# Wider DMA transfers and one decay product in a delta-rule recurrence with two MoE stages behind it

## Chip, cores and metric

One core of a Trainium2 chip. The metric is the device time of one execution in microseconds (us). Before the change it is 1340.9 us, the median of 3 runs (1339.5 to 1342.97). Engines are named as the profile does: PE (matmul; PEld loads its weights), DVE (VectorE), ACT (ScalarE), POOL (GpSimd), SP (SyncE, which here only issues transfers).

## What is computed

The reference runs a recurrence over 768 time steps for 4 x 8 heads with a 40 x 40 state each, then a mixture of 8 experts with the top 2 of them, then a dense two-layer network:

```python
for t in range(S):                       # S = 768, D = 40
    y[:, :, t] = einsum('bhd,bhde->bhe', rt, state)
    Sa = einsum('bhde,bhe->bhd', state, at)
    state = state * wt[:, :, None, :] - einsum('bhd,bhe->bhde', Sa, bt)
    state = state + einsum('bhd,bhe->bhde', vt, kt)
x = y as (B * S, H * D) = (3072, 320)
x = moe(x)                               # softmax of the top 2 noisy logits, relu experts, d_ff 1024
out = (h * tanh(softplus(h))) @ w_out    # h = x @ w_in, d_ff 2048
```

## The kernel before

The recurrence is done in 24 chunks of C = 32 time steps. For each chunk `i`, `scale` (lines 217 to 243) forms on DVE the running products E of the decays w (a scan, line 224), their counterpart R (lines 227 and 228), then `abd`, the vectors a times E (line 235), and on POOL it multiplies k and b by R in place (`kb`, line 238). Two heads share the 128 partitions: one stands on rows 0 to 39, the other on rows 64 to 103 (`RW` = 104), the rows between hold zeros. `abd` holds each head in a plane of its own (index `ab`) with zeros in the rows of the other, so a product over all 104 rows gives one head's result. For chunks 0 to 3 (`nd` = 3) DVE makes abd, later POOL does, in two products of 40 x 512.

`prods` (lines 265 to 283) multiplies abd with k and b on PE: 8 head pairs times 4 products of 32 x 64, each over 104 rows, into four column strips of one PSUM bank. ACT copies the two halves out; one, `Ls`, is stored to DRAM as `lscr`. `turns` (289 to 313) transposes kb and the decays `Ec` on PE; ACT copies the first out as `kn`, which SP stores to DRAM as `knd` (line 303), and `load_kb` (469) later reads it back as the lower half of `KB`. `kn` has two buffers.

For each group of four chunks, `solve_group` (388 to 467) loads lscr as `Lu`, inverts 128 unit triangular 32 x 32 matrices at once, mostly on DVE (lines 414 to 429), and stores them as `tscr`, which `tbd` reads back in four transfers. `apply` (365) uses them for `Zt` (line 378). The chain (lines 586 to 620) then takes 48 steps (24 chunks times two of the four batches' pairs): `u_mm`, `s_mm`, `tr`, `rv_mm` and `y_mm`, each needing the state `ST` of the step before. `rv_mm` ends with DVE's `RR` (line 584), which `y_mm` reads (line 503).

The order on PE, ACT, DVE and POOL is the order in which the program emits it: `run` walks the chain and, between its parts, `pump` emits the next piece of preparing, solving and applying whose due time has come. Each engine works its list in order. SP's list is sorted by the scheduler; it issues nearly all transfers of this part, so a load that waits for its buffer holds up what is behind it. `pair` (line 199) splits the loads of wa (w and a) and kb: one transfer for chunks 0 to 3, later one for each head's 40 rows. Four buffers hold wa for chunks 0 to 3, two later; kb has three.

The experts and the dense network (from line 1100 on) begin as the chain ends; the change does not touch them.

Of the kernel before, what the change touches and what calls it, by code (L numbers as in the profile page):

```python
# [21 lines left out]
C = 32  # L22
# [7 lines left out]
NTB = 2  # L30
GJ = 4
RW = 64 + D


def layout_rec(inp):

    c = np.ascontiguousarray

    def heads_t(x):
        return x.reshape(NP, PR, 2, NC, C, D).transpose(3, 2, 5, 1, 0, 4)  # L40


    wa = np.zeros((NC, 2, 64, NW + 1 + 2 * PR * C), np.float32)
    w33 = np.ones((NC, 2, 64, PR, 2, C + 1), np.float32)
    w33[..., 0] = 0
    w33[:, :, :D, :, :, 1:] = heads_t(inp["w"])
    wa[..., :NW] = w33.reshape(NC, 2, 64, NW)
    wa[:, :, :D, NW + 1:] = heads_t(inp["a"]).reshape(NC, 2, D, -1)
    at = inp["a"].reshape(NP, PR, 2, NC, C, D).transpose(3, 0, 4, 2, 1, 5)
    kb = np.zeros((NC, 2, 64, PR, 2, 2, C), np.float32)  # L50
    for x, n in enumerate("kb"):
        kb[:, :, :D, :, :, x] = heads_t(inp[n])
    rt = inp["r"].reshape(NP, HH, NC, C, D).transpose(2, 4, 0, 1, 3)
    vn = np.zeros((NC, NP, C, HH, 64), np.float32)
    vn[..., :D] = inp["v"].reshape(NP, HH, NC, C, D).transpose(2, 0, 3, 1, 4)
    flat = lambda x: x.reshape(NC, 128, -1)
    rows = lambda x: c(flat(x)[:, :64 + D])
    return dict(wa=rows(wa), at=c(at).reshape(NC, 64, -1), kb=flat(kb), r=c(heads_t(inp["r"])).reshape(NC, 2, D, -1), rt=c(rt).reshape(NC, D, -1), vn=vn)


UR = (96, 32)
# [2 lines left out]
class Rec:  # L64
# [22 lines left out]
    def consts_a(self):  # L87
        nc, one = self.nc, self.one
        self.w33, self.wa, self.a, self.abd, self.kb = [], [], [], [], []

        self.kbs = [one.tile([128, 4 * HH * D], F32, name=f"KB{i}") for i in range(2)]
        n = NW + 1 + 2 * PR * C
        for i in range(4):
            t = one.tile([128, n], F32, name=f"wa{i}") if i < 2 else self.kbs[0][:, n * (i - 2):n * (i - 1)]
            self.wa.append(t)
            self.w33.append(t[0:RW, 0:NW + 1])
            self.a.append(t[:, NW + 1:].rearrange("p (a b c) -> p a b c", a=PR, b=2))
        for i in range(3):
            self.kb.append(one.tile([128, PR, 2, 2, C], F32, name=f"kb{i}"))
        self.kb3 = self.share[:, 6 * PR * 96:6 * PR * 96 + 4 * PR * C].rearrange("p (a b s c) -> p a b s c", a=PR, b=2, s=2)  # L100
        self.AT = one.tile([128, 2, PR, D], F32, name="AT")
        for i in range(GJ):
            self.load_w(i)
            self.load(i)
        self.zero = one.tile([128, 64], F32, name="zero")
        nc.gpsimd.memset(self.zero, 0.0)
        self.d1 = one.tile([128, 2 * PR, C + 1], F32, name="d1")
        nc.gpsimd.memset(self.d1, 0.0)
        nc.gpsimd.memset(self.d1[:, :, 0:1], -1.0)
        self.d1b = []  # L110
        for i in range(2):
            t = one.tile([128, 2 * PR * (C + 1) + 1], F32, name=f"d1b{i}")
            nc.vector.memset(t, 0.0)
            self.d1b.append(t)
            self.abd.append(one.tile([128, PR, 2, 2, C], F32, name=f"abd{i}"))
            nc.vector.memset(self.abd[i], 0.0)
        make_identity(nc, self.ident)

        self.mml = one.tile([128, C], F32, name="mml")
        nc.gpsimd.memset(self.mml, 0.0)  # L120
        for q in range(4):
            m = self.mml[32 * q:32 * q + 32]
            nc.gpsimd.affine_select(out=m, in_=m, pattern=[[1, C]], compare_op=ALU.is_ge,
                                    fill=1.0, base=0, channel_multiplier=-1)
        self.AM = [self.share[:, i * PR * 96:(i + 1) * PR * 96].rearrange("p (a x) -> p a x", x=96)
                   for i in range(2 * GJ)]
# [69 lines left out]
                nc.vector.memset(self.kbs[i][0:64], 0.0)  # L196


    def pair(self, out, x, i, rows=RW):

        for r in (slice(0, rows),) if i < GJ else (slice(0, D), slice(64, RW)):
            self.nc.sync.dma_start(out=out[r], in_=self.ins[x][i, r])

    def load_w(self, i):
# [7 lines left out]

    def load(self, i):

        self.pair(self.kbt(i).rearrange("p a b s c -> p (a b s c)"), "kb", i, rows=RW if i >= GJ else 128)

    def scale(self, i):

        nc = self.nc
        w, a, abd, kb = self.w33[self.wx(i)], self.a[self.wx(i)], self.abd[i % 2], self.kbt(i)[0:RW]  # L220
        E = self.p2.tile([128, PR, 2, C + 1], F32, name="E")
        R = self.p2.tile([128, NW + 2], F32, name="R")
        fl = E.rearrange("p a b c -> p (a b c)")
        nc.vector.tensor_tensor_scan(out=fl[0:RW], data0=w[:, 0:NW], data1=self.d1[0:RW].rearrange("p a b -> p (a b)"),
                                     initial=0.0, op0=ALU.mult, op1=ALU.add)
        d1b = self.d1b[i % 2]
        nc.vector.reciprocal(out=d1b[0:RW, C + 1::C + 1], in_=fl[0:RW, C::C + 1])
        nc.vector.tensor_tensor_scan(out=R[0:RW, NW::-1], data0=w[:, ::-1], data1=d1b[0:RW, ::-1],
                                     initial=0.0, op0=ALU.mult, op1=ALU.add)
        yield  # L230
        m = lambda t: t.rearrange("p a b s c -> p (a b) s c")
        Rv = R[0:RW, 2:NW + 2].rearrange("p (a c) -> p a c", c=C + 1)[:, :, None, 0:C]
        for ab in range(2):
            r = slice(64 * ab, 64 * ab + D)
            (nc.vector if i <= OPT['nd'] else nc.gpsimd).tensor_tensor(out=abd[r, :, :, ab], in0=a[r], in1=E[r, :, :, 0:C], op=ALU.mult)
        if GJ <= i + 2 < len(self.seq):
            self.load_w(i + 2)
        nc.gpsimd.tensor_tensor(out=m(kb), in0=m(kb), in1=Rv.to_broadcast([RW, 2 * PR, 2, C]), op=ALU.mult)
        we = self.pwe.tile([64, 2, PR, 2], F32, name="WE")
        nc.scalar.copy(out=we[0:D, :, :, 0].rearrange("p c a -> p a c"), in_=E[0:D, :, :, C])  # L240
        nc.scalar.copy(out=we[0:D, :, :, 1].rearrange("p c a -> p a c"), in_=E[64:64 + D, :, :, C])
        self.WE[i] = we
        self.scaled[i] = E
# [21 lines left out]
    def prods(self, i):  # L265
        self.made = i + 1

        nc = self.nc
        abd, kb, am = self.abd[i % 2][0:RW], self.kbt(i)[0:RW], self.AM[i % (2 * GJ)]
        fl = lambda t: t.rearrange("p s c -> p (s c)")  # L270
        if i % GJ == 0:
            self.lscr[i // GJ] = self.pd.tile([GJ * PR, 4, C, C], F32, name="lscr")
        pt = self.pp.tile([128, 512], F32, name="pp")
        for p in range(PR):
            for q in range(4):
                ab, c = divmod(q, 2)
                nc.tensor.matmul(pt[32 * q:32 * q + 32, p * 64:p * 64 + 64], lhsT=abd[:, p, c, ab], rhs=fl(kb[:, p, c]),
                                 start=True, stop=True, tile_position=(0, 32 * q))
        ls = self.p2.tile([128, PR, C], F32, name="Ls")

        for out, k in ((ls, 1), (am[:, :, 64:96], 0)):
            nc.scalar.mul(out=out, in_=pt.rearrange("p (q s x) -> p q s x", s=2, x=C)[:, :, k], mul=-1.0)
        (nc.scalar if i < OPT['dl'] else nc.sync).dma_start(out=self.lscr[i // GJ][i % GJ * PR:i % GJ * PR + PR].rearrange("u q t i -> (q t) u i"), in_=ls)
# [5 lines left out]
    def turns(self, i):  # L289
# [6 lines left out]
        for sg in range(2):  # L296
# [2 lines left out]
            for p in range(4):  # L299
                flip(pt[:, p * 128:p * 128 + RW], kb[0:RW, sg * 4 + p].rearrange("p b s c -> p (b s c)"))  # L300
            nc.scalar.copy(out=kn[:, sg * 8:sg * 8 + 8], in_=half(pt))
        self.KN[i] = self.pkn.tile([64, 2 * HH * D], F32, name="knd")
        (nc.scalar if i < OPT['dk'] else nc.sync).dma_start(out=self.KN[i].rearrange("r (c x) -> c r x", c=2), in_=kn.rearrange("p h d -> p (h d)"))
        if i % 2 == 0:
            self.EN[i // 2] = self.pen.tile([128, 2, PR, D], F32, name="EN")
        en, r0 = self.EN[i // 2], 64 * (i % 2)
# [162 lines left out]
    def load_kb(self, i):  # L469

        KB, kn = self.KB[i % 2], self.KN.pop(i)
        self.nc.sync.dma_start(out=KB[64:128, :, 0].rearrange("p c h d -> p c (h d)"), in_=kn.rearrange("p (c x) -> p c x", c=2))

    def copy_kb(self, g):
        t = self.KB[(g // NP) % 2][64:128, g % NP]
# [7 lines left out]

    def load_r(self, i):
        nc, ins = self.nc, self.ins
        nc.sync.dma_start(out=self.R2[i % 2][0:D].rearrange("p c h t -> p (c h t)"), in_=ins["rt"][i])

    def load_rbd(self, i):
        nc, ins = self.nc, self.ins
        if True:  # L490
            for ab in range(2):
                nc.sync.dma_start(out=self.rbd[i % 2][64 * ab:64 * ab + D, ab].rearrange("p a b c -> p (a b c)"), in_=ins["r"][i, ab])

    def y_mm(self, g, sg):
        nc = self.nc
# [1211 lines left out]
```

## Time and profile before

| | us |
|---|---|
| median of 3 runs | 1340.9 |
| profiled execution | 1343.39 |
| its span | 1341.6 |
| PE busy in the span | 1160.1 (86%) |
| DVE busy | 870.0 (65%) |
| ACT busy | 704.2 (52%) |
| POOL busy | 647.1 (48%) |

Three parts can be told apart: the start, until the first product of L378 at 111.16 us; the chain of 48 steps, until some 520 us; then the experts and the dense network, where PE is the bound. Shares of the whole span mix these three, so the stretches are read one by one. A granted clock of 1.00 is 2.4 GHz, 0.50 is 1.2 GHz. A DMA share of 1 means that all 16 DMA engines of the core are busy.

### The profile page before, as it was taken

Reading aid. Unit: us, or ns where it says so; the run is one execution under the profiler, and the core shown is the slowest. Engines: PE = TensorE matmul, PEld = TensorE weight load, DVE = VectorE, ACT = ScalarE, POOL = GpSimd, SP = SyncE. Lnnn points to the kernel's source line nnn. Section 1 sums busy time; section 2 is a strip of 40 time slices with the busy share of each in tenths; the row PEclk is TensorE's granted clock in tenths of the full one; section 3 lists DMA queues with packets and bytes.
Section 4 is the critical chain, followed back from the end, with each engine's and each line's share of the span. In section 5 each row is a group of like instructions: output and inputs, shape, how many; then the busy total and the mean of one; then the engine's idle time right before and its main releaser. Section 6 shows DMA issues by size and latency. Waiting matters only on the chain. (4 is left out here: it accounts for less than half of the span.)

```text
span 1341.6 us, 34128 instructions
## 1 busy us (share of the span) xinstructions
PE 1160.1 (86%) x13902; PEld 1111.0 (83%) x13902; DVE 870.0 (65%) x1579; ACT 704.2 (52%) x1477; POOL 647.1 (48%) x575
## 2 busy tenths in 40 slices
PE   3436787988688888899999999898889999999998
PEld 2335776877577877798999999898889999999998
DVE  8585939777594742755787786777356655666543
ACT  3423665756556555442443443443266676766664
POOL 4673855747473505542244443433256454554331
PEclk9657898989889988899999999999999999999999
DMA  5444465555525648463545645635281111110000
GB/s 147 144 122 124 131 173 148 148 159 151 143 81 128 112 98 123 127 177 120 153 122 159 188 143 170 216 104 180 72 216 31 31 41 40 30 31 16 16 11 21
DMA packets 140898, 152.48 MB, mean 114 GB/s; under 512 B 69646, under 2 KB 112654, under 8 KB 140718
## 3 DMA queue, kind: packets, MB, share of 16 engines
q1 hardware_dynamic: 123502, 116.17, 32.5%
q0 software_dynamic: 10752, 22.32, 6.1%
q10 hardware_dynamic: 6464, 11.54, 3.1%
q8 instruction: 120, 1.97, 0.7%
q14 instruction: 60, 0.49, 0.1%
HBM read 106.85 MB, written 43.12 MB: 112 GB/s over the span
## 5 line engine op out<-in xcount | busy, mean ns | idle before, releaser
L1579 POOL TENSOR_TENSOR gl<-fh,gh 128x1024 fp32r<-128x1024 f32 x46 | 131.0, 2876 | 105.2 <-ACT gh L1595 101.9
L1234 PE MATMUL ph<-xh,w1h 128*128 128x256 f32 (+1 forms) x576 | 160.9, 292 | 11.6 <-issue 10.5
L1234 PE MATMUL ph<-xl,w1h 128*128 128x256 f32 (+1 forms) x576 | 160.5, 291 | 0.0
L1547 PE MATMUL fps<-fxh,ih 128*128 128x256 f32 x576 | 156.3, 286 | 1.9 <-DVE fh L1549 1.9
L1547 PE MATMUL fps<-fxl,ih 128*128 128x256 f32 x576 | 153.7, 281 | 0.5 <-DVE fxl L1090 0.3
L1578 DVE TENSOR_TENSOR fh<-fh,fp 128x1024 f32<-128x1024 f32 x48 | 95.0, 2014 | 60.3 <-ACT fp L1577 60.3
L1253 PE MATMUL py<-w2h,hh 128*128 128x320 f32 x400 | 129.9, 325 | 2.7 <-ACT hh L1086 1.9
L1253 PE MATMUL py<-w2l,hh 128*128 128x320 f32 x400 | 125.7, 314 | 2.0 <-DVE w2l L1090 1.9
L1253 PE MATMUL py<-w2h,hl 128*128 128x320 f32 x400 | 125.9, 315 | 1.3 <-DVE hl L1088 1.3
L1088 DVE SCALAR_TENSOR_TENSOR hl<-ph,hh 128x512 fp32r<-128x512 f32 (+1 forms) x104 | 69.2, 665 | 87.5 <-ACT hh L1086 87.2
L1234 PEld LDWEIGHTS ph<-xh,w1h 128*128 128x128 f32 x576 | 112.4, 195 | 12.7 <-issue 12.6
L1549 DVE COPY fh<-fps 128x512 f32<-128x512 f32 x96 | 64.8, 689 | 79.4 <-ACT fp L1548 74.1
L1609 PE MATMUL fpy<-oh,gl 128*128 128x320 f32 x384 | 114.6, 310 | 0.0
L1609 PE MATMUL fpy<-oh,gh 128*128 128x320 f32 x384 | 114.3, 310 | 0.0
L1609 PE MATMUL fpy<-ol,gh 128*128 128x320 f32 x384 | 113.9, 308 | 0.0
L1234 PEld LDWEIGHTS ph<-xl,w1h 128*128 128x128 f32 x576 | 112.5, 195 | 0.4 <-DVE xl L1090 0.3
L1234 PE MATMUL ph<-xh,w1l 128*128 128x256 f32 (+1 forms) x384 | 111.7, 291 | 0.4 <-DVE w1l L1090 0.4
L1547 PEld LDWEIGHTS fps<-fxh,ih 128*128 128x128 f32 x576 | 109.0, 189 | 2.3 <-DVE fh L1549 2.2
L1547 PEld LDWEIGHTS fps<-fxl,ih 128*128 128x128 f32 x576 | 109.0, 189 | 1.1 <-DVE fxl L1090 1.1
L1547 PE MATMUL fps<-fxh,il 128*128 128x256 f32 x384 | 107.8, 281 | 0.0
L1086 ACT ACTIVATE hh<-ph 128x512 fp32r<-128x512 f32 (+1 forms) x104 | 60.0, 581 | 90.9 <-PE ph L1234 89.9
L1548 ACT ACTIVATE fp<-fps 128x512 f32<-128x512 f32 x96 | 56.1, 597 | 79.0 <-PE fps L1547 74.9
(273 smaller groups left out, 3342.1 us busy)
## 6 DMA issues: line engine op xcount, KB each, us to landing
share<-in_w_dram SPq DMA_DIRECT2D x9, 1280.0 KB
share<-in_w_dram SPq DMA_DIRECT2D x9, 1024.0 KB
knd<-kn SPq DMA_DIRECT2D x24, 320.0 KB
KB<-knd SPq DMA_DIRECT2D x24, 320.0 KB
yb<-y SPq DMA_DIRECT2D x22, 320.0 KB
wa<-in_wa_dram SPq DMA_DIRECT2D x40, 162.7 KB
kb<-in_kb_dram SPq DMA_DIRECT2D x40, 160.0 KB
ST<-in_vn_dram SPq DMA_DIRECT2D x48, 128.0 KB
```

Of the source, the lines that this page charges most:

```text
L1086: nc.scalar.activation(out=hi, in_=src, func=AF.Relu if relu else AF.Copy)
L1088: nc.vector.scalar_tensor_tensor(out=lo, in0=src, scalar=0.0, in1=hi.bitcast(F32), op0=ALU.max, op1=ALU.subtract)
L1234: nc.tensor.matmul(ph[:, m % c], lhsT=a, rhs=b, start=(q == 0), stop=(q == len(ops) - 1))
L1253: nc.tensor.matmul(py, lhsT=a[:, m, ts], rhs=b[:, m], start=(m == 0 and q == 0), stop=(m == FC - 1 and q == 2))
L1547: nc.tensor.matmul(ph[:, i], lhsT=a, rhs=b, start=(q == 0), stop=(q == len(ops) - 1))
L1548: nc.scalar.activation(out=p[:, 2 * m2:2 * m2 + 2], in_=ph, func=AF.Sigmoid, scale=-1.0)
L1549: nc.vector.tensor_copy(h[:, 2 * m2:2 * m2 + 2], ph)
L1578: mul = lambda s: nc.vector.tensor_tensor(out=h[:, s], in0=h[:, s], in1=p[:, s], op=ALU.mult)
L1579: low = lambda s: (nc.vector if last and s.start % 8 else nc.gpsimd).tensor_tensor(out=gl[:, s], in0=h[:, s], in1=gh[:, s].bitcast(F32), o ...
L1609: nc.tensor.matmul(py, lhsT=a[:, m, ts], rhs=w[:, m], start=(q == 0), stop=(q == len(ops) - 1))
```

## The change

The store of `knd` has 128 rows of 640 numbers on both sides; before, its outermost size was 2 (the two chunks halves `c`), with 64 rows below it. `load_kb` reads it with `c` taken from the rows. The loads of wa, kb, r and rt carry 48 rows for each head (`DL` = 48) in place of 40, the additional ones zeros, and the four loads of wa in the head 112 rows in place of 104. `abd` has no planes any more: one product over all 104 rows makes it, on DVE for every chunk. `prods` multiplies each head's own 40 rows, at row 0 or 64.

```diff
+DL = 48
-    rows = lambda x: c(flat(x)[:, :64 + D])
+    rows = lambda x: c(flat(x)[:, :64 + DL])
+    pad = lambda x: np.concatenate([c(x), np.zeros((*x.shape[:-4], DL - D, *x.shape[-3:]), np.float32)], -4)
...
-            self.abd.append(one.tile([128, PR, 2, 2, C], F32, name=f"abd{i}"))
-            nc.vector.memset(self.abd[i], 0.0)
+            self.abd.append(one.tile([128, PR, 2, C], F32, name=f"abd{i}"))
...
-    def pair(self, out, x, i, rows=RW):
-        for r in (slice(0, rows),) if i < GJ else (slice(0, D), slice(64, RW)):
+    def pair(self, out, x, i, rows=64 + DL):
+        for r in (slice(0, rows),) if i < GJ else (slice(0, DL), slice(64, 64 + DL)):
...
-        for ab in range(2):
-            r = slice(64 * ab, 64 * ab + D)
-            (nc.vector if i <= OPT['nd'] else nc.gpsimd).tensor_tensor(out=abd[r, :, :, ab], in0=a[r], in1=E[r, :, :, 0:C], op=ALU.mult)
+        nc.vector.tensor_tensor(out=abd[0:RW], in0=a[0:RW], in1=E[0:RW, :, :, 0:C], op=ALU.mult)
...
-        abd, kb, am = self.abd[i % 2][0:RW], self.kbt(i)[0:RW], self.AM[i % (2 * GJ)]
+        abd, kb, am = self.abd[i % 2], self.kbt(i), self.AM[i % (2 * GJ)]
...
-                nc.tensor.matmul(pt[32 * q:32 * q + 32, p * 64:p * 64 + 64], lhsT=abd[:, p, c, ab], rhs=fl(kb[:, p, c]),
-                                 start=True, stop=True, tile_position=(0, 32 * q))
+                r = slice(64 * ab, 64 * ab + D)
+                nc.tensor.matmul(pt[32 * q:32 * q + 32, p * 64:p * 64 + 64], lhsT=abd[r, p, c], rhs=fl(kb[r, p, c]),
+                                 start=True, stop=True, tile_position=(64 * ab, 32 * q))
...
-        self.KN[i] = self.pkn.tile([64, 2 * HH * D], F32, name="knd")
-        (nc.scalar if i < OPT['dk'] else nc.sync).dma_start(out=self.KN[i].rearrange("r (c x) -> c r x", c=2), in_=kn.rearrange("p h d -> p (h d)"))
+        self.KN[i] = self.pkn.tile([128, HH * D], F32, name="knd")
+        (nc.scalar if i < OPT['dk'] else nc.sync).dma_start(out=self.KN[i], in_=kn.rearrange("p h d -> p (h d)"))
...
-        self.nc.sync.dma_start(out=KB[64:128, :, 0].rearrange("p c h d -> p c (h d)"), in_=kn.rearrange("p (c x) -> p c x", c=2))
+        self.nc.sync.dma_start(out=KB[64:128, :, 0].rearrange("p c h d -> p c (h d)"), in_=kn.rearrange("(c p) x -> p c x", c=2))
```

`load_r` and `load_rbd` load `DL` rows in place of `D` in the same way.

How the lists move: on DVE a product for abd follows each R. The piece is DVE's list around the scans of chunks 4 and 5, in the start; `wa`, `d` and `d1b` are inputs of the scans, `P` and `tm` belong to the solving. Before:

```order
L224 SCALAR_TENSOR_TENSOR E<-wa_139,d_155 104x528
L227 RECIPROCAL d1b_158<-E 104x16
L228 SCALAR_TENSOR_TENSOR R<-wa_139,d1b_158 104x529
L429 TENSOR_REDUCE P<-tm 128x64
L224 SCALAR_TENSOR_TENSOR E<-wa_140,d_155 104x528
L227 RECIPROCAL d1b_162<-E 104x16
L228 SCALAR_TENSOR_TENSOR R<-wa_140,d1b_162 104x529
```

The same place with the change:

```order
L225 SCALAR_TENSOR_TENSOR E<-wa_139,d_155 104x528
L228 RECIPROCAL d1b_158<-E 104x16
L229 SCALAR_TENSOR_TENSOR R<-wa_139,d1b_158 104x529
L234 TENSOR_TENSOR abd_160<-wa_139,E 104x512
L429 TENSOR_REDUCE P<-tm 128x64
L225 SCALAR_TENSOR_TENSOR E<-wa_140,d_155 104x528
L228 RECIPROCAL d1b_161<-E 104x16
L229 SCALAR_TENSOR_TENSOR R<-wa_140,d1b_161 104x529
```

Only the row of L234 is new; the rest of DVE's list keeps its order.

On POOL both products of each chunk go. The piece is POOL's list from the end of the head to chunk 6; `share` is the tile that holds the decayed a of `scale_a` (L262) and the masked products (L287). Before:

```order
L287 TENSOR_TENSOR share<-share,mml 128x8x32 x4
L262 TENSOR_TENSOR share<-AT,EN 64x8x40 x6
L235 TENSOR_TENSOR abd_160<-wa_139,E 40x16x32 x2
L238 TENSOR_TENSOR kb_142<-kb_142,R 104x1024
L262 TENSOR_TENSOR share<-AT,EN 64x8x40 x2
L131 MEMSET share 128x16x24
L235 TENSOR_TENSOR abd_164<-wa_140,E 40x16x32 x2
L238 TENSOR_TENSOR kb_143<-kb_143,R 104x1024
```

The same place with the change:

```order
L287 TENSOR_TENSOR share<-share,mml 128x8x32 x4
L261 TENSOR_TENSOR share<-AT,EN 64x8x40 x6
L237 TENSOR_TENSOR kb_142<-kb_142,R 104x1024
L261 TENSOR_TENSOR share<-AT,EN 64x8x40 x2
L132 MEMSET share 128x16x24
L237 TENSOR_TENSOR kb_143<-kb_143,R 104x1024
```

The kb products (L238, now L237) stand directly behind `scale_a`. The lists of PE, ACT and SP keep their order.

## Rows read from the trace of the kernel before

**Rows 1.** The page, the span in 40 equal slices, PE and its clock
```profile
PE   3436787988688888899999999898889999999998
...
PEclk9657898989889988899999999999999999999999
```
**Rows 2.** Stretches (us): busy time of each engine, granted clock, DMA share, GB/s
```profile
core 0: us, PE busy (x) PEld busy (x) DVE busy (x) ACT busy (x) POOL busy (x), PEclk, DMA share, GB/s
...
111.00:530.00 419.00, 348.13 (x7488) 316.60 (x7488) 279.52 (x471) 252.68 (x700) 228.29 (x195) 0.90 0.56 134
530.00:1342.00 812.00, 772.84 (x5793) 763.17 (x5792) 511.02 (x1029) 414.48 (x693) 347.95 (x282) 0.98 0.35 100
```
**Rows 3.** Short stretches of the start, same columns
```profile
17.50:18.00 0.50, 0.37 (x12) 0.14 (x12) 0.47 (x2) 0.00 (x0) 0.00 (x0) 1.00 0.77 251
23.00:23.50 0.50, 0.09 (x2) 0.09 (x4) 0.50 (x1) 0.00 (x0) 0.36 (x1) 1.00 0.61 242
...
61.00:64.00 3.00, 1.62 (x8) 1.06 (x7) 0.00 (x0) 0.61 (x2) 2.54 (x3) 0.50 0.13 51
```
**Rows 4.** Timeline of SP's transfers in the start: issue, us, what
```profile
99.02 0.36 SPq L463 DMA_DIRECT2D tscr<-Tt  x1
99.47 0.57 SPq L303 DMA_DIRECT2D knd<-kn  x1
```
**Rows 5.** Waits of the start (total us, times, longest), and PE's first L378
```profile
DVE E L224 <- DMA wa<-in_wa_dram: 13.1, 1, 13.1
DVE E L224 <- ACT Ec L248: 3.2, 1, 3.2
ACT kn L301 <- DMA knd<-kn: 12.1, 5, 4.7
...
111.16 3.70 PE L378 MATMUL pp<-Tbd,share 128*96 128x128 f32 x16 [14.19 <-DMA kb<-in_kb_dram]
```
**Rows 6.** PE's waits from 111 to 530 us: total us, times, longest
```profile
PE pp L378 <- DMA Tbd<-tscr: 10.7, 4, 4.5
PE cs L528 <- issue: 8.3, 2, 4.7
PE cs L528 <- DMA ST<-in_vn_dram: 8.1, 3, 3.7
PE cs L528 <- DVE RR L584: 7.3, 5, 2.3
...
PE Y L503 <- DVE RR L584: 5.1, 3, 2.6
```
**Rows 7.** Timeline from 193 to 207 us, PE and DVE
```profile
193.93 1.31 PE L503 MATMUL Y<-KB,RR 128*32 128x40 f32 x32
...
202.86 0.17 DVE L414 TENSOR_TENSOR tm<-Tt,Lu 128x4 f32<-128x4 f32 x1 [10.94 <-DMA Lu<-lscr]
...
206.59 2.34 PE L503 MATMUL Y<-KB,RR 128*32 128x40 f32 x32 [2.61 <-DVE RR L584]
```
**Rows 8.** Groups by line and shape: busy us, mean ns | idle before
```profile
L235 POOL TENSOR_TENSOR abd<-wa,E 40x512 f32<-40x512 f32 x40 | 62.4, 1560 | 33.5 <-DMA ST<-in_vn_dram 16.1 <-PE cs L558 9.4 <-PE cs L541 2.1
...
L228 DVE TENSOR_TENSOR_SCAN R<-wa,d1b 104x529 f32<-104x529 f32 x22 | 40.5, 1841 | 1.5
...
L228 DVE TENSOR_TENSOR_SCAN R<-KB,d1b 104x529 f32<-104x529 f32 x2 | 2.5, 1259 | 0.2
```
**Rows 9.** Timeline of chunk 3: both abd, and POOL's kb
```profile
26.77 0.66 DVE L235 TENSOR_TENSOR abd<-KB,E 40x512 f32<-40x512 f32 x1
...
27.46 2.55 DVE L235 TENSOR_TENSOR abd<-KB,E 40x512 f32<-40x512 f32 x1
...
26.93 2.52 POOL L238 TENSOR_TENSOR share<-share,R 104x1024 f32<-104x1024 f32 x1 [3.57 <-DVE R L228]
```
**Rows 10.** L's products on PE: the group, and one block
```profile
L277 PE MATMUL pp<-kb,abd 104*32 104x64 f32 x1472 | 32.9, 250 | 35.1 <-POOL kb L238 34.8
...
190.54 1.10 PE L277 MATMUL pp<-kb,abd 104*32 104x64 f32 x64
```

More of the change, by code (lines that the diff above doesn't have):

```diff
@@ L56, in layout_rec @@
     flat = lambda x: x.reshape(NC, 128, -1)
-    rows = lambda x: c(flat(x)[:, :64 + D])
-    return dict(wa=rows(wa), at=c(at).reshape(NC, 64, -1), kb=flat(kb), r=c(heads_t(inp["r"])).reshape(NC, 2, D, -1), rt=c(rt).reshape(NC, D, -1), vn=vn)
+    rows = lambda x: c(flat(x)[:, :64 + DL])
+    pad = lambda x: np.concatenate([c(x), np.zeros((*x.shape[:-4], DL - D, *x.shape[-3:]), np.float32)], -4)
+    return dict(wa=rows(wa), at=c(at).reshape(NC, 64, -1), kb=flat(kb), r=pad(heads_t(inp["r"])).reshape(NC, 2, DL, -1), rt=pad(rt).reshape(NC, DL, -1), vn=vn)
 UR = (96, 32)
@@ L213, in load @@
     def load(self, i):
-        self.pair(self.kbt(i).rearrange("p a b s c -> p (a b s c)"), "kb", i, rows=RW if i >= GJ else 128)
+        self.pair(self.kbt(i).rearrange("p a b s c -> p (a b s c)"), "kb", i, rows=128)
     def scale(self, i):
@@ L485, in load_r @@
         nc, ins = self.nc, self.ins
-        nc.sync.dma_start(out=self.R2[i % 2][0:D].rearrange("p c h t -> p (c h t)"), in_=ins["rt"][i])
+        nc.sync.dma_start(out=self.R2[i % 2][0:DL].rearrange("p c h t -> p (c h t)"), in_=ins["rt"][i])
     def load_rbd(self, i):
@@ L491, in load_rbd @@
             for ab in range(2):
-                nc.sync.dma_start(out=self.rbd[i % 2][64 * ab:64 * ab + D, ab].rearrange("p a b c -> p (a b c)"), in_=ins["r"][i, ab])
+                nc.sync.dma_start(out=self.rbd[i % 2][64 * ab:64 * ab + DL, ab].rearrange("p a b c -> p (a b c)"), in_=ins["r"][i, ab])
     def y_mm(self, g, sg):
```

## The prediction

> **What bounds the kernel now.** I read the 40 slices of 33.5 us first [rows 1]: from the 18th on PE is mostly busy at 0.9 and more; in the first four it is at 0.3 to 0.6, and its clock falls to 0.5; between them it is at 0.6 to 0.9. The stretches say the same in microseconds [rows 2]: from 530 us to the end PE works 772.84 of 812 us, and none of that work is touched. From 111 to 530 us (the 48 steps of the chain) it works 348.13 of 419 us at a mean clock of 0.90, so some 71 us are idle. So what the change is worth is decided before 530 us, and what is won there moves the rest forward as a whole.
>
> What the early part waits for stands in the DMA share. From 61 to 64 us, as in other stretches behind the stores of **knd**, the share is 0.13 at 51 GB/s [rows 3]: 0.13 of 16 engines is two engines, at some 25 GB/s each. A store of 320 KB at 51 GB/s takes 327,680 B / 51 GB/s = **6.4 us**, there are 24 of them, 154 us in all, and every later transfer that also needs those two engines stands behind. The loads of 40 rows show the same thing milder: while only they run, share 0.61 and 242 GB/s [rows 3], that is ten engines. The waits name who pays [rows 5]: in the start VectorE waits 13.1 us for a load of `wa`, and 3.2 us for ScalarE's copy `Ec`, which itself sits behind `kn` copies that wait 12.1 us for knd stores. PE's first product of the chain waits 14.2 us, up to 111.16 us [rows 5], though its source `tscr` was stored at 99.02; directly behind that store SP issued a knd store [rows 4].
>
> **The change, part by part. knd over all engines.** Both sides of the store are now 128 rows of 2,560 B. The nearest row for a wide transfer is that of the head [rows 3]: 251 GB/s at a share of 0.77. At that rate a store takes 1.3 us in place of 6.4. The bounds: 51 GB/s (nothing changes) and 16 x 25 = 400 GB/s (0.8 us). I take 1.3, since the other transfers share the engines. The 40-row loads become 48-row loads: a fifth more bytes, but three rows on each of 16 engines in place of four on each of ten, if 48 spreads over 16, which no row shows. The Trainium skill, "DMA: Bandwidth & Descriptors", section "Why a DMA increments its semaphore by 16 and not by 1", says that the engine count is the largest up to 16 that divides the outermost sizes; by it 48 and 128 go over 16, and two engines for knd and ten for 40 rows agree with the shares above.
>
> *The start.* VectorE's waits of 13.1 and 3.2 us are 16.3 [rows 5]. The wa load will be issued at about the same place in SP's list, whose order does not change, and land behind one knd store: 1.3 us, and 1.6 for its own 400 KB at 251 GB/s, so I keep 3 us of wait: **-13**. From tscr's store to PE's start it took 111.16 - 99.02 = 12.1 us, with one knd store among the transfers between; it gives back at most 6.4 - 1.3 = 5.1, and I take **-3.5**. Bounds for both: 0, if POOL or ScalarE is as late, and -16.3 - 5.1.
>
> *The chain.* From 111 to 530 us PE's waits with a transfer at the end are 10.7 us for Tbd and 8.1 for ST [rows 6]; the 8.3 of "issue" may be transfers too, for nothing that the profile shows was missing. One more is a DMA in disguise: at 202.86 us VectorE gets Lu after 10.94 us and begins the L414 ladder; the RR product that PE wants stands behind it, PE is idle 2.61 us up to 206.59, and then the 32 products L503 take 2.34 us where they took 1.31 at 193.93 [rows 7]: after the hole PE runs at its lower clock. RR is 7.3 + 5.1 us of PE's waits [rows 6]. So 10.7 + 8.1 = 19 us are sure to belong to DMA, 8 more are likely and 12 possible: 39; and the lower clock behind a hole costs about 1 us for each block like that of L503, perhaps 18 us over six large holes with three such blocks each (an estimate). Bounds 0 and 39 + 18; I take **-26**, the 19 sure ones and 7 of the rest, since the next thing (POOL's kb, ScalarE's copies) will be late at some of these places.
>
> **abd in one product, on VectorE.** Per stage, two POOL products of 1.56 us go (62.4 us in all [rows 8]) and VectorE gets one of 104x512. On VectorE two of 40x512 stand in each of the first four stages; the first takes 0.66 us, the second 2.55 [rows 9]: the second begins beside POOL's kb product (26.93, 2.52 us) and ends when that has ended. The new one is like the first, for it stands directly behind R, and kb waits for R too: 20 x 0.66 = 13 us added. Against it stands R: 1.26 us in the head, where POOL makes no abd, and a mean of 1.84 over the 22 others [rows 8]; without abd on POOL it falls by 0.58 x 20 = 11.6. Sum on VectorE **0**; bounds +51 (20 abd behind a kb, 2.55 each) and -12. That POOL's 62 us go is worth nothing by itself, since POOL works 228.29 of 419 us in the chain [rows 2] and is waited for seldom; but kb comes two abd, some 3 us, earlier in each stage. If kb takes its turn first, the next late thing is RR, and PE waits for it.
>
> *The head.* VectorE is busy throughout a stage of the head, with E, R and two abd. One abd goes, but E of the next stage now meets kb as the second abd did, so only the first one's 0.66 us is sure; bounds 0.66 and 2.55 [rows 9] a stage, for three stages. I take the lower: **-2**. The two memsets of abd stood while wa was awaited: nothing.
>
> **L's products on 40 rows.** 32 products a stage stay 32, each on 40 rows at row 0 or 64 in place of 104. A block of 64 instructions takes 1.10 us, though an instruction takes 250 ns in the mean [rows 10]: they overlap over four column strips. No row shows a product that starts at row 64. Fewer rows do not shorten a product whose columns are the same: **0**. The Trainium skill says against it ("TensorEngine Tiling (Array Packing)", section "Restrictions and Gotchas") that different row tiles cannot access the same PSUM bank at the same time; here both halves write one bank. By rows 10 the sum stays; by that rule it is the slow rival below.
>
> **Sum.** -13 - 3.5 - 26 + 0 - 2 + 0 = **-44.5**. The profiled execution took 1343.39 us (span 1341.6 and 1.8 around it), 2.5 above the median of 1340.9; 1343.4 - 44.5 = 1299. Against the median it would be 1296. I say **1298**.
>
> **The rivals.**
> - *Only the start gains* (0.17). The chain's order is fixed, and each hole closed by a faster store may open again for ScalarE, VectorE or POOL; for it: PE's 12.4 us of waits for RR [rows 6] and VectorE at 279.52 of 419 us [rows 2]. Then -18.5: 1325.
> - *All holes close and the clock with them* (0.15). For it: the clock of 0.90 in the chain against 0.98 later [rows 2]. Start -21, chain -39, clock -18, head -2: 1343 - 80 = 1263, say 1270 with something left.
> - *Slower: the halves take turns in PSUM* (0.08). Place: the 16 stages whose products lie in the chain. Each block changes its row half 16 times; if each change waits for an instruction to end (250 ns [rows 10]), a block costs 16 x 0.25 = 4.0 us more, 64 us in the chain, where PE is the bound, with the other 8 blocks hidden in the start. 1299 + 64 = 1363. It decides from 44.5 / 16 = 2.8 us a block. Against it: the halves use different columns and partitions.
> - *The stores do not spread* (0.04). Both sides must have 128 rows outermost as issued; if not, 1341: only the head gains 2 us.
>
> **How the numbers follow.** The forecast has 0.56, with a range of its own of 1283 to 1314; with all holes closed 0.15, only the start 0.17, slower 0.08, no spread 0.04. The range that leaves out no more than 2 in 10 takes in 'only the start' and most of 'all holes': **1268 to 1328**. A measurement of this kernel tells about 0.3%, 4 us, from no change. Faster 0.88, same 0.04, slower 0.08.
>
> **What would show it.** Right: no stretch at share 0.13 and 51 GB/s in the first 500 us; VectorE's wait for wa under 4 us; the first product of L378 near 92 us in place of 111; ScalarE's wait for knd gone; R near 1.26 us and abd on VectorE near 0.66; the block of L's products still 1.1 us at full clock; the gap between the first L378 and the end smaller by some 26 us. Wrong: a block over 2.8 us; abd over 2 us with PE's waits for RR above 12 us; new waits on PE for kb or `share` that take the place of those for Tbd and ST.

## The result, and the profile after

The changed kernel takes **1309.64 us** (median of 4 runs, 1307.29 to 1311.88), the kernel before beside it 1341.93: a ratio of **0.9755** [0.9722, 0.9789]. The direction and the range of the prediction hold; 1298 was 12 us too low. The profiled execution took 1308.13 us (span 1306.3) in place of 1343.39: 35.3 us less, where the sum said 44.5.

The page of the changed kernel, the 40 slices (now of 32.7 us), PE and its clock:

```profile
PE   3538888889789787998999999899989999999998
PEclk9559989999889799999999999889999999999999
```

Its stretches (columns as in [rows 2]). The third stands near the end of the chain and is needed further down:

```profile
61.00:64.00 3.00, 2.37 (x12) 1.81 (x12) 3.00 (x4) 1.69 (x6) 2.01 (x2) 0.50 0.39 123
...
111.00:530.00 419.00, 357.58 (x7485) 324.87 (x7482) 299.36 (x533) 260.36 (x721) 199.62 (x182) 0.91 0.63 146
...
474.00:498.00 24.00, 20.58 (x341) 18.16 (x340) 4.81 (x11) 13.01 (x38) 11.91 (x23) 0.86 1.01 156
```

From 61 to 64 us, where [rows 3] had a share of 0.13 at 51 GB/s, it is now 0.39 at 123 GB/s, and VectorE works through all 3 us (though this is work that came later in the kernel before). In slices of 1 us from the beginning to 520 us, 40 slices of the kernel before lie at a share of 0.11 to 0.14 with 46 to 55 GB/s, and one slice of the changed kernel does. The stretch from 111 to 530 us can't be set against [rows 2] as it stands, since the changed kernel's chain already ends at 496.5 us. Over the chain alone (its bounds follow below) PE works 342.00 of 411.43 us before and 337.59 of 392.19 after, VectorE 275.82 and 282.98: PE is idle 14.8 us less, and VectorE has more to do. The waits (columns as in [rows 5, 6]: the start, then PE from 111 to 530 us):

```profile
DVE E L225 <- DMA wa<-in_wa_dram: 2.3, 1, 2.3
ACT kn L301 <- DMA knd<-kn: 0.8, 1, 0.8
...
PE cs L528 <- DVE RR L584: 12.0, 4, 3.9
PE pp L378 <- DMA Tbd<-tscr: 8.9, 3, 4.7
PE Y L503 <- DVE RR L584: 2.8, 1, 2.8
```

Against [rows 5, 6]: `wa` 13.1 to 2.3 (without the wait for the first load, at 5 us: 1.6 before, 3.3 after) and knd 12.1 to 0.8; PE's wait for ST (8.1) is gone, that for Tbd is nearly what it was (10.7), and that for RR is 14.8 in place of 12.4. PE's waits for ScalarE's copies of L's products (`share`, L282), as large as these, hardly change: 12.7 us before, 11.3 after. The 12.4 is too low, though, since one wait for RR stands under "issue" in the trace of before (timeline, DVE and PE):

```profile
230.87 3.48 DVE L228 TENSOR_TENSOR_SCAN R<-wa,d1b 104x529 f32<-104x529 f32 x1
...
234.38 0.86 DVE L584 TENSOR_TENSOR RR<-cs,mrv 64x256 f32<-64x256 f32 x2
...
235.34 0.77 PE L528 MATMUL cs<-ST,Zt 128*32 128x40 f32 x32 [3.60 <-issue]
```

R, slow beside a product on POOL, ends at 234.35, RR at 235.24, and PE goes on at once. With it the waits for RR are 16.0 before and 14.8 after. The groups (columns as in [rows 8, 10]):

```profile
L229 DVE TENSOR_TENSOR_SCAN R<-wa,d1b 104x529 f32<-104x529 f32 x22 | 32.2, 1465 | 1.5
L277 PE MATMUL pp<-kb,abd 40*32 40x64 f32 x1472 | 31.8, 246 | 23.9 <-POOL kb L237 23.4 <-issue 0.2
L234 DVE TENSOR_TENSOR abd<-wa,E 104x512 f32<-104x512 f32 x22 | 29.2, 1328 | 0.0
L234 DVE TENSOR_TENSOR abd<-KB,E 104x512 f32<-104x512 f32 x2 | 1.3, 667 | 0.0
```

The last line is the price that was forecast (0.66 us). The line above it, where nearly all of them stand, has twice that in the mean: half of its 22 products take under 1 us, four take 2.4 to 3.35. The timeline of the changed kernel (start, us, engine) shows the start, one block of L's products, one abd of the chain, and the first and last L573 of the chain:

```profile
36.86 0.20 DVE L414 TENSOR_TENSOR tm<-Tt,Lu 128x4 f32<-128x4 f32 x1 [4.01 <-DMA Lu<-lscr]
...
86.84 0.34 SPq L463 DMA_DIRECT2D tscr<-Tt  x1
...
89.48 1.83 SPq L361 DMA_DIRECT2D Tbd<-tscr  x4
...
93.47 3.70 PE L378 MATMUL pp<-Tbd,share 128*96 128x128 f32 x16 [14.82 <-DMA Tbd<-tscr]
...
104.34 0.98 PE L573 MATMUL cs<-rbd,TRs 128*64 128x64 f32 x16
...
205.27 1.10 PE L277 MATMUL pp<-kb,abd 40*32 40x64 f32 x64
...
207.86 3.60 DVE L426 TENSOR_TENSOR tm<-Tt,P 128x1024 f32<-128x1024 f32 x1
...
209.62 3.85 POOL L237 TENSOR_TENSOR kb<-kb,R 104x1024 f32<-104x1024 f32 x1
...
211.37 3.33 DVE L234 TENSOR_TENSOR abd<-wa,E 104x512 f32<-104x512 f32 x1
...
218.85 1.08 PE L528 MATMUL cs<-ST,Zt 128*32 128x40 f32 x26 [3.90 <-DVE RR L584]
...
495.84 0.69 PE L573 MATMUL cs<-rbd,TRs 128*64 128x64 f32 x16
```

and of the kernel before its first and last L573:

```profile
122.03 0.98 PE L573 MATMUL cs<-rbd,TRs 128*64 128x64 f32 x16
...
532.77 0.69 PE L573 MATMUL cs<-rbd,TRs 128*64 128x64 f32 x16
```

The first L378 comes 17.7 us earlier (111.16 [rows 5] to 93.47). From the first to the end of the last L573, called the chain below, it is 411.4 us before (up to 533.5 us, not some 520 as said ahead) and 392.2 after: 19.2 less. The two make 36.9; in the experts and the dense network, which the change does not touch, 1.6 are lost again.

### The profile page after: what moved, and what is told of

Its sections match the earlier page's. It is cut to its first block, busy times and chain, and to the rows that moved or that the text cites. A ratio compares the mean times of both kernels' runs of the same rounds, so it can differ in the third digit from the quotient of the medians.

```text
span 1306.3 us, 34038 instructions
## 1 busy us (share of the span) xinstructions
PE 1154.5 (88%) x13902; PEld 1106.0 (85%) x13902; DVE 873.7 (67%) x1593; ACT 703.4 (54%) x1477; POOL 593.8 (45%) x535
## 5 line engine op out<-in xcount | busy, mean ns | idle before, releaser
L1234 PEld LDWEIGHTS ph<-xh,w1h 128*128 128x128 f32 x576 | 113.1, 196 | 10.6 <-issue 10.4
L261 POOL TENSOR_TENSOR share<-AT,EN 64x320 f32<-64x320 f32 x48 | 60.7, 1264 | 82.9 <-ACT EN L312 57.6
```

The lines of the kernel that those rows point to most:

```text
L261: self.nc.gpsimd.tensor_tensor(out=self.AM[i % (2 * GJ)][64 * ab:64 * ab + 64, :, 0:D], in0=self.AT[r, ab], in1=en[r, ab], op=ALU.mult)
L1234: nc.tensor.matmul(ph[:, m % c], lhsT=a, rhs=b, start=(q == 0), stop=(q == len(ops) - 1))
```

## Experiments

Each batch ran on one chip with the kernel before beside it: 1345.28 us there in the first (17 runs), 1344.62 in the second (13), 1366.08 in the third (11). "Ratio" is against that, in brackets its 95% interval; "first L378", "chain" and the waits for RR, with those listed as "issue" (3.6 us before, 8.1 in g4_solve_earlier), are of the one profiled run, in us. The only profile of the kernel before is that of the first row, from none of these batches, and the chain of the changed kernel itself is 392, 402 and 413 us in its three profiles; so chains are best compared within a batch.

| run | us (runs) | ratio | first L378 | chain | PE waits for RR |
|---|---|---|---|---|---|
| before | 1341.93 (4) | 1 | 111.16 | 411 | 16.0 |
| changed | 1309.64 (4) | 0.9755 [0.9722, 0.9789] | 93.47 | 392 | 14.8 |
| e1_knd_only | 1317.30 (4) | 0.9783 [0.9747, 0.982] | 99.42 | 401 | 11.4 |
| e2_knd_two_engines | 1352.84 (10) | 1.0055 [1.003, 1.0079] | 109.96 | 425 | 18.8 |
| e3_abd_behind_R | 1307.25 (6) | 0.9705 [0.9671, 0.974] | 93.66 | 392 | 9.8 |
| e4_abd_one_on_pool | 1313.07 (6) | 0.9754 [0.9725, 0.9783] | 95.63 | 403 | 13.2 |
| c1_changed_again | 1318.77 (4) | 0.9811 [0.9749, 0.9872] | 93.89 | 402 | 16.7 |
| e5_forty_rows | 1311.71 (4) | 0.9763 [0.9705, 0.9821] | 93.48 | 396 | 14.0 |
| e6_all_dma_old_products | 1322.87 (4) | 0.9824 [0.9763, 0.9885] | 98.46 | 404 | 10.4 |
| e7_old_dma_new_products | 1349.45 (10) | 1.0042 [1.002, 1.0064] | 109.58 | 418 | 17.3 |
| c2_changed_control | 1332.35 (6) | 0.9752 [0.9709, 0.9795] | 93.74 | 413 | 13.6 |
| g2_abd_behind_R_again | 1325.70 (6) | 0.9706 [0.9662, 0.9749] | 94.07 | 408 | 9.7 |
| g3_abd_behind_R_forty_rows | 1324.12 (6) | 0.9697 [0.9654, 0.9741] | 94.73 | 406 | 6.0 |
| g4_solve_earlier | 1326.06 (6) | 0.9709 [0.9669, 0.975] | 94.20 | 412 | 13.3 |

The theory was that the spread store carries the gain and that abd on VectorE costs nothing; the rivals were that the loads of 48 rows, or POOL without abd, carry it.

**The store alone.** Only the store of knd and its read are changed:

```diff
-        self.KN[i] = self.pkn.tile([64, 2 * HH * D], F32, name="knd")
+        self.KN[i] = self.pkn.tile([128, HH * D], F32, name="knd")
...
-out=self.KN[i].rearrange("r (c x) -> c r x", c=2)
+out=self.KN[i]
...
-in_=kn.rearrange("p (c x) -> p c x", c=2)
+in_=kn.rearrange("(c p) x -> p c x", c=2)
```

> The kernel before, with the knd store (and its load) alone as in the change: 128 rows outermost. Theory (the two-engine store held nearly all of the gain): the stretches at share 0.13 and 51 GB/s are gone, VectorE's wait for wa falls from 13.1 us to under 4, the first product of L378 is at 94 to 97 us (before 111.16, with the change 93.47), the time is 1308 to 1318 us. Rival (abd's move to VectorE and the wider loads held half of it): first L378 above 100 us, time 1320 to 1330 us.

It takes 0.9783 alone, most of what the change gives. The time is in the theory's range; the first L378 lies between what the theory and the rival said. VectorE's wait for `wa` is 2.1 us, nearly as after, and no slice of 1 us is left at 0.11 to 0.14 with 46 to 55 GB/s. The read of knd changes with the store, and no run tells the two apart; the low rate stood behind the stores. The start gains 11.7 us of the 17.7. The other 6 stand in its timeline:

```profile
84.45 3.83 POOL L235 TENSOR_TENSOR abd<-wa,E 40x512 f32<-40x512 f32 x2
88.36 2.18 POOL L238 TENSOR_TENSOR kb<-kb,R 104x1024 f32<-104x1024 f32 x1
...
90.09 0.35 SPq L463 DMA_DIRECT2D tscr<-Tt  x1
90.53 0.38 SPq L303 DMA_DIRECT2D knd<-kn  x1
...
92.15 2.74 POOL L262 TENSOR_TENSOR share<-AT,EN 64x320 f32<-64x320 f32 x2
...
94.92 0.47 SPq L255 DMA_DIRECT2D AT<-in_at_dram  x1
96.01 1.81 SPq L361 DMA_DIRECT2D Tbd<-tscr  x4
```

tscr is issued 3.3 us later than after, and Tbd 5.9 us behind it in place of 2.6. Between the two SP issues the load of `AT`, at 94.92: `AT` is free when POOL's L262 ends at 94.89, and that product stands behind two abd and kb. After, POOL has no abd, and the same load needs no waiting (87.75). That is where POOL's freed time pays: through SP's list. But not all of the 6 us is POOL's: with abd as one product on POOL (below, the rest as in the change), the same load does not wait (89.07) and the first L378 is at 95.63. So some 2 us hang on POOL having no abd; the other 3.8 come with the rest of the change, one product in place of two among it.

**The other way round.** The changed kernel with the old store (the edit above, backwards), and the kernel before with abd and L's products as in the change, all transfers as before (the old store, and `DL = 40`):

> The changed kernel with the knd store as before (outermost size 2). Theory: the store fills two engines for 6.4 us again, share 0.13 at 51 GB/s behind each, first L378 at 106 to 112 us, time 1332 to 1342 us. Rival (the other parts held half of the gain): 1318 to 1328 us.

> The kernel before with abd in one product on VectorE and L's products on 40 rows, all transfers as before. Theory (with the store on two engines VectorE's abd comes on top of the late transfers in the chain): slower than before, 1346 to 1356 us, the chain from the first to the last L573 over 418 us. Rival (it was the loads of 48 rows that cost, there): 1332 to 1342 us.

Both are slower than before, by 0.55% and 0.42%, with intervals above 1. The first is slower than its theory and its rival said. The second is where its theory put it, and its rival falls: with the loads of 40 rows the loss stays. The start hardly moves (109.96, 109.58), VectorE waits 12.6 and 12.4 us for `wa` again, and the chain is 14 and 7 us longer than in the profile of before. In the second, the group of abd and PE's waits:

```profile
L234 DVE TENSOR_TENSOR abd<-wa,E 104x512 f32<-104x512 f32 x22 | 30.9, 1404 | 0.0
...
PE cs L528 <- DVE RR L584: 11.8, 4, 3.9
PE Y L503 <- DVE RR L584: 5.5, 3, 2.7
```

So the new abd and products, as the change places them, are a cost in the chain when nothing else is changed. PE's waits for RR grow by only 1 to 3 us (16.0 to 17.3 and 18.8); the rest of the loss has no single wait to show. The two runs don't tell abd from the 40-row products.

**All transfers, old abd and products.**

```diff
...
-        nc.vector.tensor_tensor(out=abd[0:RW], in0=a[0:RW], in1=E[0:RW, :, :, 0:C], op=ALU.mult)
+        for ab in range(2):
+            r = slice(64 * ab, 64 * ab + D)
+            (nc.vector if i <= OPT['nd'] else nc.gpsimd).tensor_tensor(out=abd[r, :, :, ab], in0=a[r], in1=E[r, :, :, 0:C], op=ALU.mult)
...
-                nc.tensor.matmul(pt[32 * q:32 * q + 32, p * 64:p * 64 + 64], lhsT=abd[r, p, c], rhs=fl(kb[r, p, c]),
+                nc.tensor.matmul(pt[32 * q:32 * q + 32, p * 64:p * 64 + 64], lhsT=abd[:, p, c, ab], rhs=fl(kb[:, p, c]),
```

> The changed kernel's transfers (knd over 128 rows, loads of 48 rows) with abd in two products, on POOL from chunk 4 on, and L's products over 104 rows, as before. Theory (the store carries the gain, abd and the products add a little): 1311 to 1318 us, 3 to 9 above the changed kernel, the chain from the first to the last L573 some 400 us as with the store alone. Rival (abd's move costs, as the run with the store on two engines suggests): below the changed kernel, 1296 to 1304 us.

The start is that of the store alone (98.46). Against the changed kernel of its batch the time is 1.0019 [0.998, 1.0059] of it (worked out from the runs of both, as all ratios between two runs below): what abd and the products win in the start (5 us), is not seen at the end. The rival falls. The medians are 4.1 us apart, as the theory had it, but the interval does not tell that from nothing. Its waits for RR are 10.4 us, those of the changed kernel in that batch 16.7.

**48 rows or 40.** The changed kernel with

```diff
-DL = 48
+DL = 40
```

and, beside it, the changed kernel itself:

> The changed kernel with loads of 40 rows for each head (104 rows for the four of wa in the head) in place of 48 (112). Theory (the loads of 48 rows are worth little, for loads of 40 already go over ten engines at 242 GB/s): within 5 us of the changed kernel, first L378 at 93 to 96 us. Rival (the additional six engines matter beside the other transfers): 8 us or more above it, first L378 above 98 us.

> The changed kernel itself, unchanged, on the same chip as the next three, so that they can be compared with it: ratio to before 0.972 to 0.979, some 1308 to 1316 us. No theory is at stake.

With 40 rows it is 0.9947 [0.9915, 0.9979] of the changed kernel, with the same start. The third batch asks again (below) and finds no difference. The rival falls: the 48 rows win nothing. Whether a fifth more bytes cost a little is not settled.

**abd directly behind R.** In the change a place where other work may be emitted stands between R and abd. Here abd is emitted ahead of it:

```diff
+        nc.vector.tensor_tensor(out=abd[0:RW], in0=a[0:RW], in1=E[0:RW, :, :, 0:C], op=ALU.mult)
...
-        nc.vector.tensor_tensor(out=abd[0:RW], in0=a[0:RW], in1=E[0:RW, :, :, 0:C], op=ALU.mult)
```

> The changed kernel with the abd product emitted ahead of the yield, so that it stands directly behind R on VectorE everywhere, not only in the start. Theory (in the chain kb on POOL begins first and abd, then RR, stand behind it): abd falls from a mean of 1.33 us to under 0.9, no abd over 2 us, PE's waits for RR from 14.8 us to under 9, time 4 to 8 us under the changed kernel: 1300 to 1305 us. Rival (RR is late because of the solve's products L426, whatever abd does): waits for RR stay above 12 us, time within 3 us of the changed kernel.

Its group of abd, and PE's waits for RR:

```profile
L231 DVE TENSOR_TENSOR abd<-wa,E 104x512 f32<-104x512 f32 x22 | 20.4, 928 | 0.0
...
PE cs L528 <- DVE RR L584: 5.2, 3, 1.9
PE Y L503 <- DVE RR L584: 4.6, 3, 2.5
```

abd costs 20.4 us in place of 29.2, the waits for RR are 9.8 in place of 14.8. Each falls a little short of the theory (under 0.9 us a product, under 9 us, 1300 to 1305 us), and one product of 3.33 us is left; the rival's waits over 12 us are not there. Against the store alone, in the same batch, the time is 0.9918 [0.9881, 0.9955]. Whether it is also faster than the changed kernel was left to the third batch.

**abd in one product, but on POOL** from chunk 4 on:

```diff
-        nc.vector.tensor_tensor(out=abd[0:RW], in0=a[0:RW], in1=E[0:RW, :, :, 0:C], op=ALU.mult)
+        (nc.vector if i <= OPT['nd'] else nc.gpsimd).tensor_tensor(out=abd[0:RW], in0=a[0:RW], in1=E[0:RW, :, :, 0:C], op=ALU.mult)
```

> The changed kernel with abd as one product of 104x512 on POOL for chunks 4 to 23, on VectorE only for chunks 0 to 3 as before. Theory (VectorE's additional 20 us in the chain are partly on the path): PE's waits for RR under 10 us, R back at a mean of 1.6 to 1.8 us, time 1302 to 1307 us. Rival (kb behind abd on POOL makes the products of L late): new PE waits for kb, time 1310 to 1316 us.

The 20 products take 1474 ns each on POOL, R is back at 1754, and the first L378 comes 2 us later than after. The theory falls: the waits for RR are 13.2 us, not under 10, and the time is in the rival's range, though PE's new waits for kb, by which the rival explained it, are 0.4 us in all. At 0.9754 it can't be told from the changed kernel (0.9755 and 0.9811 on two other chips), nor from the store alone (0.9979 [0.9937, 1.0021]); abd directly behind R is 0.994 [0.9894, 0.9985] of it.

**The best order, and the waits for Tbd.** The third batch ran the changed kernel again, abd behind R, the same with `DL = 40`, and that with the solving of a group spread over a shorter time:

```diff
-s=(.05, .72)
+s=(.05, .64)
```

> The changed kernel once more, as the measure for the other three runs on the same chip. Both theories: 1307 to 1319 us (what two batches gave), first product of the chain at 93.5 us, waits of TensorE for RR in the chain of 14 to 17 us.

> abd directly behind R, now beside the changed kernel on the same chip. Theory (the late abd and RR of the chain cost VectorE 8 to 9 us and TensorE some 5): 4 to 8 us below the control of this batch, the waits for RR near 10 us. Rival (the 10 us by which the chain differs between runs of one kernel is all there was): within 2 us of the control.

> abd directly behind R, and loads of 40 rows as before. Theory (the spread store is the whole gain, 48 rows are worth nothing): within 2 us of the run with abd behind R alone, so below the control by 4 to 8 us; waits of VectorE for wa still under 3 us. Rival (48 rows hold the chain's transfers on time): 3 us or more above that run, waits for wa back over 5 us.

> As the run before, and a group's solve spread over 0.05 to 0.64 of the time in place of 0.05 to 0.72. Theory (the waits for Tbd late in the chain are the round trip of tscr, which starts too late): the waits for Tbd fall from about 9 us to under 4, and the time is 3 to 6 us below the run with 40 rows. Rival (the rows of the solve crowd the products that RR stands behind): the waits for RR rise by as much, and the time is the same or above.

The control's time is above what was expected, as is that of the kernel before on this chip; its waits for RR, 13.6 us, are just below. abd behind R is 0.9949 [0.9915, 0.9983] of the control, 6.7 us by the medians, as the theory had it; with 40 rows it is 0.9993 [0.9957, 1.0028] of that. By the ratios to before these two, 0.9706 and 0.9697, are the best versions. The waits for `wa` with 40 rows are 7.2 us over the whole run, where the control has 3.2: more than the theory's 3 and the rival's 5, but without the rival's price in the time.

The theory of the solve fell, and its rival holds. The waits for Tbd do disappear from PE's waits, but the time is 1.0013 [0.9985, 1.0042] of the run before it. There was less to win than the expectation had: its 9 us are those of the first profile, and the run before has 0.9 us of them, with 2.9 more at the same product put down to a load of RR. PE's largest waits in its chain now stand under "issue" (14.1 us in the run before). The line, and the place of the longest (timeline, DVE and PE):

```profile
PE cs L528 <- issue: 23.3, 18, 4.1
```

```profile
209.30 3.25 DVE L231 TENSOR_TENSOR abd<-wa,E 104x512 f32<-104x512 f32 x1
...
212.58 0.86 DVE L584 TENSOR_TENSOR RR<-cs,mrv 64x256 f32<-64x256 f32 x2
...
213.54 1.21 PE L528 MATMUL cs<-ST,Zt 128*32 128x40 f32 x30 [4.13 <-issue]
```

PE goes on where RR has ended, so this is a wait for RR, as is another of 3.93 us: 8.1 us under a wrong name, 13.3 in all against 6.0. At this place abd stands beside POOL's product of the solve (L426, from 208.34 to 212.00), and it is slow again although it stands behind R.

Most of the other "issue" waits are something else. The control shows it near the end of its chain (a stretch, with the columns of [rows 2], then lines of the timeline, PE and POOL):

```profile
474.00:498.00 24.00, 9.85 (x121) 7.06 (x119) 2.22 (x7) 2.28 (x8) 16.64 (x31) 0.61 0.23 35
```

```profile
489.06 0.23 PE L528 MATMUL cs<-ST,Zt 128*32 128x40 f32 x1 [1.11 <-issue]
489.78 0.26 PE L528 MATMUL cs<-ST,Zt 128*32 128x40 f32 x1 [0.49 <-issue]
...
489.36 0.96 POOL L980 DMA_INDIRECT ids<-tok,POS  x1 [0.23 <-issue]
```

PE issues a product or two every 0.7 to 1.4 us for some 20 us, while POOL issues scatter after scatter of `ids` (L980), part of the routing for the experts and untouched by the change. The first run of the changed kernel had 341 products in the same 24 us (the third stretch above) and five such holes, from 481 to 487 us. PE works 10.7 us less in this stretch. From the start of the 44th L573 to the end of the 48th and last it is 42.1 us in the control and 27.8 in that first profile: 14.3 of the 20 us by which the control's chain is longer. The other kernels of the third batch show the same (some 195 products in 27 us with abd behind R, 315 in the first batch). Whether it is the scatters that hold PE up, and how, is not shown: they stand beside the holes, and a run without them was not tried.

## Why the prediction was right, and where it was wrong

*The start* (forecast -18.5, measured -17.7). The total is right by luck, for its parts are not. The two waits of 16.3 us became 2.3, as said (3 left), but tscr is issued 12.2 us earlier where the sum had 15 (13 and the head's 2), and PE begins 6.6 us behind it in place of 12.1: 5.5 less, where 3.5 was taken and 5.1 was the bound. The store alone gives 11.7 of the forecast 16.5 (13 and 3.5): where the transfers are on time, `AT` is late behind POOL's abd. Of the other 6, some 2 come from abd off POOL and the rest with the other parts of the change, of which only the head's 2 were forecast. The first L414 is indeed 2.0 us earlier (38.83 to 36.86), and E of the head takes 3.2 us beside kb, as feared. The step that failed here is "POOL's 62 us go is worth nothing by itself": they had stood covered behind SP's list, which was late because of the stores.

*The chain, transfers* (forecast -26). The store alone took 10 us off the chain (411 to 401), the changed kernel 19 in its first profile, 10 in the second and none in the third (413). Up to the start of the 44th L573, ahead of most of the holes beside the scatters, the chain takes 381.9 us before, 370.6 with the store alone, and 364.4, 371.3 and 370.5 with the change: 11 to 17 us of the 26, with no profile of before on the later chips. The term's size was too large, and 19.2 in the first profile is the best of three. Of the "19 sure ones" only ST's 8.1 went. **Tbd's 10.7 did not belong to the slow store**: 8.9 remain, the two largest at the same two steps late in the chain, and the other profiles of the changed kernel have 7.4 and 3.3, that of the store alone 14.4. At the second tscr is issued at 424.06, SP issues Tbd only at 435.00, and the 16 engines were busy (share 1.02 at 124 GB/s from 424 to 434 us); what SP waited for there is not shown. The step "8 more are likely" failed too: of the 8.3 us of "issue" 3.6 were the wait for RR shown above, and the other 4.7, at 523 us, stand among the scatters of `ids`: the first was no transfer, the cause of the other is not shown. Of the 12 "possible" ones of RR (16.0 with the hidden one) 4.6 went with the store alone (11.4), and with abd on VectorE most of them were back (14.8).

*abd on VectorE* (forecast 0). **This is the step that was wrong by kind**: "it stands directly behind R" holds in the start, where the trace of order was read, and not in the chain. There other work comes between, POOL's kb starts first, and abd waits for it: in the timeline kb runs from 209.62 to 213.47 and abd from 211.37 to 214.70, 3.33 us for a product of 0.66. RR, and with it PE, come behind: 3.90 us at 218.85. All of abd, E and R on VectorE took 89.2 us before and takes 101.9 after; R fell by 8.3 of the forecast 11.6, abd rose by 17.7 in place of 11 (13 less the 2 of the head). Put behind R, it gains 0.5%; there the waits for RR are 9.7 us against the control's 13.6. The Trainium skill ("SBUF — State Buffer", section "Who interferes with whom") says that a VectorE operation with two inputs in SBUF contends with a GpSimd operation that reads SBUF, that the shared ports are an exclusive lock, and that the order of issue decides who waits. The trace agrees in both directions, to some 0.6 us: L426 ends at 211.46, and kb, begun under it, takes 3.85 us in place of 2.5 (after L426 alone it would have ended at 213.96, and it ended at 213.47); abd, 0.66 us alone, ends 1.23 us behind kb.

*L's products* (forecast 0). Right: the block takes 1.10 us as before [rows 10], the group 246 ns in place of 250, so the slow rival never came near its 2.8 us a block. The restriction on row tiles in one PSUM bank, cited in the prediction from the Trainium skill ("TensorEngine Tiling (Array Packing)", section "Restrictions and Gotchas"), costs no time here. The halves of a head pair write different partitions of one bank, in strips of 32; their columns are the same, not different as the prediction has it. No run tried them on the same partitions.

*The stores spread*: the rival "do not spread" is excluded. That 48 rows would be better than 40 was priced at nothing in the sum, and is worth nothing.

The sum: of the 9 us by which the profiled time is above the sum, 7 are the chain (19.2 in place of 26), 1 the start and 1.6 the rest. "Only the start gains" (1325) was too dark by some 15 us in the first run, the forecast too bright by 12; c1's time (1318.77, ratio 0.9811) lies nearer to the former. Taken together, the spread store is what the change gains (0.9783 alone, and without it the rest is slower than before). abd and L's products add nothing to it that the times can tell (1.0019 [0.998, 1.0059] without them), unless abd stands directly behind R.

## What to carry to other kernels

A transfer on two of sixteen engines also costs what stands behind it (VectorE waited 11 us less for `wa` once the stores were spread): look for stretches with a small DMA share and a constant low rate, and put the large dimension outermost on both sides. An operation moved to VectorE has to be read at each of its places, also where other work can be emitted between it and the one that it follows: behind a GpSimd product it costs that product's rest too, and what stands behind it pays. A wait on a transfer that is listed for the bound engine is not yet the gain: read it in more than one profile (Tbd's was 8.9, 7.4 and 3.3 us in one kernel), and ask what its cure will crowd. The earlier solve took the last of these waits away, and the waits for RR grew by 7.3 us.

## What was not expected of the hardware

PE's drip of single products while POOL's indirect scatters run (121 products in 24 us against 341), with the DMA share at 0.23 and nothing in the profile that PE waits for; in its long form it came in the third batch alone, and its cause stays open. And loads of 40 rows, at a share of 0.61 in the kernel before [rows 3], ten engines of 16, cost nothing against 48 that two batches can tell. The store on two engines did; a store on ten was not tried.
